# Activation sums and split widths in the second MLP product of a talking-heads kernel

## Chip, cores and metric

One core of a Trainium2 chip runs the whole program. The metric is the device time of one execution in microseconds, the median of the timed runs.

## What is computed

Four batches (b) of attention with 12 heads, 448 positions and head width 64, whose scores and weights are mixed over the heads, are followed by a leaky MLP on the 1792 rows:

```python
scores = einsum('bhij,hg->bgij', q @ k.T / 8, w_pre)
attn = exp(scores - max); attn = attn / (sum(attn) + 1e-9)
x = einsum('bhij,hg->bgij', attn, w_post) @ v        # rows b*S, columns 768
h = x @ w_in                                         # 768 -> 2048
out = maximum(0.01 * h, h) @ w_out                   # 2048 -> 768
```

## The kernel before

Everything is float32, transposed: features lie on the 128 partitions, the 448 positions of a batch are the columns. Attention runs first (some 460 us) and leaves x in DRAM (`x_dram`), while the MLP weights are unpacked into `w_dram`.

**The MLP works on pairs of batches** (p = 0 with batches 0 and 1, p = 1 with 2 and 3). Each product of a pair is a 2 x 2 block product done with seven sub-products in place of eight (names 1 to 7, in the order 1, 2, 6, 7, 5, 4, 3), whose operands are sums and differences of blocks. Each sub-product is made in float32 precision from rounded parts: `split` (L355) has ScalarE copy an operand into a high part (`wh`, `gh`, `xh`, ...; a CAST, L359) and VectorE subtract to get the low part (`wl`, `gl`, `xl`; L360). `three` (L413) then issues three matmuls: low weights by high data, high by low, high by high. 

**First product** (`hidden`, L446): eight steps j, each with seven sub-products of 9 matmuls. Weights of a step (`wi`, L382) are combined and split in parts a, s, b, d, c (`prep_wi`, L388): `wa` for sub-products 1 and 2, `wb` for 6 and 7, `wc` for 5 and 3, `wd` for 4. `keep` (L439) applies the leaky activation on ScalarE and leaves four blocks of activations g per step, in tiles of 448 columns. In pair 0, `combine_wo` (L480) has GpSimd form the four sums of the second product's weights from a load `so` and store them to `s_dram`.

**Second product** (`project`, L534): 56 steps n (seven sub-products by eight j), 9 matmuls each (three output blocks c, three matmuls). `load_wo` (L495) loads 128 x 384 weights; `prep_out` (L507) splits them and the activations of step n + 2, and has GpSimd form the five sums of activations that the later sub-products use, one block of 448 columns at a time (L517 to L526, 40 in a pair). Three buffers hold the split activations `gs`, three the split weights. In pair 0 the x blocks of pair 1 are loaded, summed and split on VectorE between the steps (`load_x` L346, `prep_x` L363, called from step 4 on).

**What sets the order.** Matmuls stay in program order (`mm`, L159); everything else is ordered by the scheduler's estimate when the program is built, and each engine then works its own list in that order. All DMAs named here are issued by SP, also in order: an issue that waits holds up those behind it. Pools opened by `open_work` (L335) take the memory of those it closes, so their first writes wait for the last readers there.

## Time and profile before

| what | us |
|---|---|
| three timed runs | 937.64, 938.81, 945.68 (median 938.81) |
| profiled execution | 934.08 |
| its span, first to last instruction | 932.4 |

The profile is that of one execution; its stages are read by the time at which they begin and end on TensorE. PE is TensorE's matmuls, PEld its weight loads, DVE VectorE, ACT ScalarE, POOL GpSimd, SPq the queue of SP.

### The profile page before, as it was taken

Reading aid. Unit: us, or ns where it says so; the run is one execution under the profiler, and the core shown is the slowest. Engines: PE = TensorE matmul, PEld = TensorE weight load, DVE = VectorE, ACT = ScalarE, POOL = GpSimd, SP = SyncE. Lnnn points to the kernel's source line nnn. Section 1 sums busy time; section 2 is a strip of 40 time slices with the busy share of each in tenths; the row PEclk is TensorE's granted clock in tenths of the full one; section 3 lists DMA queues with packets and bytes.
Section 4 is the critical chain, followed back from the end, with each engine's and each line's share of the span. In section 5 each row is a group of like instructions: output and inputs, shape, how many; then the busy total and the mean of one; then the engine's idle time right before and its main releaser. Section 6 shows DMA issues by size and latency. Waiting matters only on the chain.

```text
span 932.4 us, 18211 instructions
## 1 busy us (share of the span) xinstructions
PE 867.1 (93%) x6712; PEld 674.9 (72%) x6712; DVE 687.0 (74%) x1234; ACT 516.4 (55%) x1167; POOL 305.4 (33%) x278
## 2 busy tenths in 40 slices
PE   7999999999999999997798999778999999977998
PEld 3557757666666666665787899556889999965997
DVE  4688878787787878888857665998685655498665
ACT  3576666656666766664434554535655545442654
POOL 2133432333332333334644431782000110198000
PEclk8999999999999999999789999999999999999999
DMA  7878778877698786866555523334451122223343
GB/s 186 232 240 264 218 222 247 277 223 235 214 280 247 232 239 212 262 200 195 184 180 202 170 68 112 106 98 124 134 169 54 53 68 68 60 74 101 106 138 118
DMA packets 111081, 158.75 MB, mean 170 GB/s; under 512 B 37180, under 2 KB 95632, under 8 KB 110992
## 3 DMA queue, kind: packets, MB, share of 16 engines
q1 hardware_dynamic: 109660, 156.04, 54.7%
q10 hardware_dynamic: 1236, 1.53, 0.5%
q8 instruction: 53, 0.87, 0.4%
q14 instruction: 36, 0.29, 0.1%
q0 software_dynamic: 96, 0.01, 0.0%
HBM read 88.09 MB, written 29.88 MB: 127 GB/s over the span
## 4 chain that ended last, share of the span: by engine, by line
PE 63%; DVE 14%; DMA 10%; ACT 5%; issue 5%; POOL 3%; SPq 1%; DVEq 0%; ACTq 0%; POOLq 0%
PE pso L160 26%; PE psa L160 10%; PE pss L160 8%; PE psh L160 7%; PE psx L160 6%; PE psm L160 5%; DVE gl L360 3%; DVE wl L360 3%; DMA craw<-in_w_moe 2%; ACT et L246 2%; DMA so<-w_dram 2%; DMA xr<-x_dram 1%; DVE xl L360 1%; DMA w_dram<-w 1%; DMA wi<-w_dram 1%
## 5 line engine op out<-in xcount | busy, mean ns | idle before, releaser
L160 PEld LDWEIGHTS psa<-kp,et 128*128 128x128 f32 (+1 forms) x1840 | 158.3, 172 | 77.2 <-ACT st L212 28.2
L160 PE MATMUL psa<-kp,et 128*128 128x120 f32 (+1 forms) x1840 | 178.7, 261 | 8.9 <-DVE at L290 3.9
L119 POOL TENSOR_TENSOR w<-w,exp 128x384 f32<-128x384 f32 x64 | 66.0, 1032 | 266.3 <-issue 93.9
L160 PE MATMUL pso<-gl,wh 128*128 128x448 f32 x336 | 127.9, 381 | 18.6 <-DVE gl L360 18.6
L246 ACT ACTIVATE et<-psm,stat 128x448 f32<-128x448 f32 x184 | 115.8, 634 | 49.8 <-DVE stat L245 49.3
L160 PE MATMUL pso<-gh,wl 128*128 128x448 f32 x336 | 125.2, 373 | 10.1 <-ACT xh L359 4.4
L160 PE MATMUL pso<-gh,wh 128*128 128x448 f32 x336 | 124.1, 369 | 0.0
L245 DVE TENSOR_REDUCE stat<-psm 128x1 f32<-128x448 f32 x184 | 105.7, 616 | 17.0 <-PE psm L160 16.7
L360 DVE TENSOR_TENSOR wl<-wo,wh 128x384 fp32r<-128x384 f32 x112 | 86.0, 773 | 41.9 <-ACT wh L359 41.8
L160 PE MATMUL pss<-kt,qt 64*64 64x448 f32 (+2 forms) x768 | 109.7, 567 | 5.7 <-ACT st L212 3.9
L359 ACT CAST wh<-wo 128x384 fp32r<-128x384 f32 x112 | 57.2, 513 | 102.9 <-PE pso L160 77.2
L160 PE MATMUL psm<-r,kpre 64*64 64x448 f32 (+1 forms) x736 | 100.6, 552 | 4.6 <-DMA r<-st 4.6
L212 ACT ACTIVATE st<-pss 120x448 f32<-120x448 f32 (+1 forms) x141 | 71.8, 545 | 50.5 <-PE pss L160 49.2
L160 PEld LDWEIGHTS pso<-gl,wh 128*128 128x128 f32 x336 | 63.9, 190 | 34.6 <-DVE gl L360 29.6
L290 DVE COPY at<-psa 128x480 f32<-128x480 f32 (+1 forms) x112 | 70.3, 632 | 19.8 <-PE psa L160 19.5
L160 PEld LDWEIGHTS pso<-gh,wl 128*128 128x128 f32 x336 | 64.0, 190 | 19.6 <-ACT gh L359 5.9
L360 DVE TENSOR_TENSOR gl<-g,gh 128x448 fp32r<-128x448 f32 x96 | 78.1, 815 | 0.0
L160 PE MATMUL psx<-at,vt 128*64 128x120 f32 (+1 forms) x1152 | 66.7, 266 | 5.5 <-ACT st L212 3.1
L160 PEld LDWEIGHTS pso<-gh,wh 128*128 128x128 f32 x336 | 64.0, 191 | 4.8
L160 PEld LDWEIGHTS psm<-r,kpre 64*64 64x64 f32 (+1 forms) x736 | 33.6, 136 | 44.5 <-issue 38.6
L120 POOL TENSOR_TENSOR w<-w,top 128x384 f32<-128x384 f32 x64 | 64.0, 1000 | 5.0
L160 PEld LDWEIGHTS psx<-at,vt 128*64 128x64 f32 x1152 | 58.0, 139 | 6.9 <-ACT st L212 3.8
(129 smaller groups left out, 1586.3 us busy)
## 6 DMA issues: line engine op xcount, KB each, us to landing
r<-st SPq DMA_DIRECT2D x182, 210.0 KB
craw<-in_w_moe SPq DMA_DIRECT2D x64, 384.0 KB
w_dram<-w SPq DMA_DIRECT2D x64, 192.0 KB
wi<-w_dram SPq DMA_DIRECT2D x32, 384.0 KB
wo<-s_dram SPq DMA_DIRECT2D x64, 192.0 KB
wo<-w_dram SPq DMA_DIRECT2D x48, 192.0 KB
so<-w_dram SPq DMA_DIRECT2D x16, 384.0 KB
s_dram<-sw SPq DMA_DIRECT2D x8, 768.0 KB
```

Source lines behind the costliest of these rows:

```text
L119: pin(nc.gpsimd.tensor_mul(w, w, self.exp.bitcast(F32)))
L120: pin(nc.gpsimd.tensor_add(w, w, self.top.bitcast(F32)))
L160: pin(nc.tensor.matmul(*args, **kw))
L212: nc.scalar.activation(to, ps[:m, :S], AF.Copy, scale=scale)
L245: nc.vector.tensor_reduce(st[:, 0, g:g + 1], ps[:, :S], axis=AX.X, op=ALU.max, negate=True)
L246: nc.scalar.activation(e, ps[:, :S], AF.Exp, bias=st[:, 0, g:g + 1], accum_out=st[:, 1, g:g + 1])
L290: copy(at[:, :, QUAD * sg[0]:QUAD * sg[0] + w], ps[:, :nh * w].rearrange("p (h w) -> p h w", h=nh))
L359: hold(nc.scalar.copy(hi, raw))
L360: hold(nc.vector.tensor_sub(lo, raw, hi.bitcast(F32)))
```

## The change

- The activations of two steps j lie in one tile of 2 x 448 columns (`keep`), and a step of the second product takes two j: 28 steps of 18 matmuls, with splits of 768 and 896 columns, two weight loads a step and two buffers each for `wr`, `w` and `gs` (one step ahead).
- The sums of activations are made by VectorE in 896 columns: one of the four in the first product (after sub-product 3 of every odd j), three behind the splits of sub-products 1, 2 and 6. GpSimd has none.
- In the first product of pair 0 (after j = 1, 3, 5) the x blocks of pair 1 are loaded, summed on VectorE (`combine_x`) and stored to `xq_dram`; in the second product `load_part` and `prep_part` load and split one of 21 blocks per step, three ahead.
- In the first product `wb` is split for sub-products 6, 7 and 5 at once (1152 columns), 4 and 3 have pools of their own (`w4`, `w3`) on the right side, where `gs` lies later.
- At the end of pair 0's second product parts b, d and c of the first weights follow; part a and s are placed at steps 16 and 20. `c` tiles have four buffers and not five.

```diff
         name, raw = ((1, x[0][0]), (2, x[1][0]), (5, t), (7, x[0][1]), (6, t), (3, x[1][1]), (4, x[1][0]))[k]
         x_t[name, c] = split(pl["xs"][X_PARTS * c + k >= XS], "x", raw, hold)
 
+    X_NAMES = (1, 2, 5, 7, 6, 3, 4)
+
+    def combine_x(c):
+        x = [[xr_t[1, c, h, e] for e in range(2)] for h in range(2)]
+        t = pl["xr"].tile([P, S], F32, tag="xr", name="xt")
+        sub = nc.vector.tensor_sub
+        sub(t, x[0][1], x[0][0])
+        nc.sync.dma_start(xq_dram[c][:, 0], t)
+        sub(x[0][1], x[1][1], x[0][1])
+        nc.sync.dma_start(xq_dram[c][:, 1], x[0][1])
+        sub(x[1][1], x[1][1], t)
+        nc.sync.dma_start(xq_dram[c][:, 2], x[1][1])
+        sub(x[1][0], x[1][0], x[1][1])
+        nc.sync.dma_start(xq_dram[c][:, 3], x[1][0])
+
+    def load_part(c, k):
+        if c >= HC:
+            return
+        name = X_NAMES[k]
+        t = xr_t[1, c, k] = pl["xr"].tile([P, S], F32, tag="xr", name="xr")
+        if name < 4:
+            src = x_dram[2 + (name == 3)][:, c + HC * (name > 1)]
+        else:
+            src = xq_dram[c][:, (5, 7, 6, 4).index(name)]
+        nc.sync.dma_start(t, src)
+
+    def prep_part(c, k):
+        x_t[X_NAMES[k], c] = split(pl["xs"][X_PARTS * c + k >= XS], "x", xr_t.pop((1, c, k)))
+
     def load_wi(j):
         t = pl["wi"].tile([P, 2, 2, HALF_IN], F32, tag="r", name="wi")
         for m in range(2):
...
             hold(nc.vector.tensor_sub(s[:, 0], s[:, 2], w[:, 0, 0]))
         if part == "b":
-            two = split(pl["wb"], "wb", wi_t["s"][:, :2], hold)
-            s_t2[6], s_t2[7] = (two, 0), (two, 1)
+            two = split(pl["wb"], "wb", wi_t["s"][:, :3], hold)
+            s_t2[6], s_t2[7], s_t2[5] = (two, 0), (two, 1), (two, 2)
         if part == "d":
             s = wi_t["s"]
             hold(nc.vector.tensor_sub(s[:, 3], w[:, 0, 1], s[:, 0]))
-            s_t2[4] = split(pl["wd"], "wd", w[:, 1, 1:], hold), 0
+            s_t2[4] = split(pl["w4"], "wd", w[:, 1, 1:], hold), 0
         if part == "c":
-            two = split(pl["wc"], "wc", wi_t["s"][:, 2:], hold)
-            s_t2[5], s_t2[3] = (two, 0), (two, 1)
+            s_t2[3] = split(pl["w3"], "wc", wi_t["s"][:, 3:], hold), 0
 
     def three(ps, w, x, first, last):
 
...
         return pl[pool].tile([P, 512], F32, tag=tag, name="psh" if pool == "ps_h" else "pso")
 
     def keep(j, m, e, h):
-        g = g_t[j, m, e] = pl["g"].tile([P, S], F32, tag=f"g{m}{e}", name=f"g{m}{e}", bufs=NJF)
-        nc.scalar.activation(g, h, AF.Prelu, alpha=0.01)
+        if j % 2 == 0:
+            g_t[j // 2, m, e] = pl["g"].tile([P, 2, S], F32, tag=f"g{m}{e}", name=f"g{m}{e}", bufs=NJF // 2)
+        nc.scalar.activation(g_t[j // 2, m, e][:, j % 2], h, AF.Prelu, alpha=0.01)
 
     NJF = NF // 2
...
         if k == 3:
             product(3, hid[1], False)
             keep(j, 0, 1, hid[1][:, :S])
+            if j % 2:
+                g = g_t[j // 2, 0, 1]
+                nc.vector.tensor_sub(g, g_t[j // 2, 1, 1], g)
...
 
     ORDER = (1, 2, 6, 7, 5, 4, 3)
-    STEPS = len(ORDER) * NJF
+    NG = NJF // 2
+    STEPS = len(ORDER) * NG
 
     def load_wo(n):
         if n >= STEPS:
             return
-        k, j = ORDER[n // NJF], n % NJF
-        t = wo_t[n] = pl["wr"].tile([P, HALF_IN], F32, tag="r", name="wo")
-        if k in (1, 2, 4):
-            src = w_dram[2 * j + (k != 1)][:, DM + HALF_IN * (k == 4):][:, :HALF_IN]
-        else:
-            at = (5, 7, 6, 3).index(k)
-            src = s_dram[j][:, HALF_IN * at:HALF_IN * (at + 1)]
-        nc.sync.dma_start(t, src)
+        k, i = ORDER[n // NG], n % NG
+        t = wo_t[n] = pl["wr"].tile([P, 2, HALF_IN], F32, tag="r", name="wo")
+        for u in range(2):
+            j = 2 * i + u
+            if k in (1, 2, 4):
+                src = w_dram[2 * j + (k != 1)][:, DM + HALF_IN * (k == 4):][:, :HALF_IN]
+            else:
+                at = (5, 7, 6, 3).index(k)
+                src = s_dram[j][:, HALF_IN * at:HALF_IN * (at + 1)]
+            nc.sync.dma_start(t[:, u], src)
 
     def prep_out(n):
         if n >= STEPS:
             return
-        k, j = ORDER[n // NJF], n % NJF
-        wq_t[n] = split(pl["w0" if n % 3 == 0 else "w1"], "w", wo_t.pop(n))
-        g = {(m, e): g_t[j, m, e] for m in range(2) for e in range(2)}
-        t = g[{1: (0, 0), 2: (1, 0), 7: (0, 1), 5: (0, 0), 4: (1, 0), 3: (1, 1)}.get(k, (0, 0))]
-        sub = nc.gpsimd.tensor_sub
+        k, i = ORDER[n // NG], n % NG
+        wq_t[n] = split(pl["w"], "w", wo_t.pop(n))
+        b11, b12, b21, b22 = (g_t[i, m, e] for m in range(2) for e in range(2))
+        gs_t[n] = split(pl["gs"], "g", {1: b11, 2: b21, 6: b11, 7: b12, 5: b11, 4: b21, 3: b22}[k])
+        if k == 1:
+            nc.vector.tensor_add(b11, b12, b11)
+        if k == 2:
+            nc.vector.tensor_sub(b21, b21, b11)
         if k == 6:
-            t = pl["t"].tile([P, S], F32, tag="t", name="gt")
-            sub(t, g[1, 1], g[0, 0])
-        gs_t[n] = split(pl["gs"], "g", t)
-        if k == 1:
-            sub(g[0, 0], g[0, 1], g[0, 0])
-        if k == 2:
-            sub(g[0, 1], g[1, 1], g[0, 1])
-        if k == 7:
-            sub(g[1, 0], g[1, 0], g[1, 1])
-        if k == 5:
...
     def project(p, n):
-        k, j = ORDER[n // NJF], n % NJF
+        k, i = ORDER[n // NG], n % NG
         own = 2 if k in (2, 7, 4) else 1
         fresh = k in (1, 2, 7)
         w, g = wq_t.pop(n), gs_t.pop(n)
-        for c in range(HC):
-            if fresh and j == 0:
+        for u, c in ((u, c) for u in range(2) for c in range(HC)):
+            first, last = fresh and i == u == 0, i == NG - 1 and u == 1
+            if first:
                 o_b[own, c] = bank("ps_o", f"b{own}")
             ps = o_b[own, c]
-            three(ps[:, :S], [t[:, c * P:(c + 1) * P] for t in w], g, fresh and j == 0, j == NJF - 1)
-            if j < NJF - 1:
+            three(ps[:, :S], [t[:, u, c * P:(c + 1) * P] for t in w], [t[:, u] for t in g], first, last)
...
                     load_wi((j + 2) % NJF)
-        open_work(
-            gs=("left", 3), w0=("left", 1), wr=("right", 3), w1=("right", 2), t=("right", 2),
-        )
-        for n in range(3):
-            load_wo(n)
-        for n in range(2):
-            prep_out(n)
+            if not p and j % 2 and j < 2 * HC:
+                load_x(1, j // 2)
+                combine_x(j // 2)
+        open_work(wr=("left", 2), w=("left", 2), gs=("right", 2))
+        load_wo(0)
+        load_wo(1)
+        prep_out(0)
+        again = p + 1 < B // 2
+        if again:
+            for k in range(3):
+                load_part(0, k)
         for n in range(STEPS):
-            load_wo(n + 3)
-            prep_out(n + 2)
+            load_wo(n + 2)
+            prep_out(n + 1)
             project(p, n)
-            if p + 1 == B // 2:
-                continue
-            c, at = divmod(n - 4, 16)
-            if 0 <= c < HC and at == 0:
-                load_x(p + 1, c)
-            if 0 <= c < HC and at > 1 and at % 2 == 0:
-                prep_x(p + 1, c, at // 2 - 1)
-            if n == 30:
+            if again and n < X_PARTS * HC:
+                load_part(*divmod(n + 3, X_PARTS))
+                prep_part(*divmod(n, X_PARTS))
+            if again and n == 16:
                 prep_wi(0, "a")
-            if n == 36:
+            if again and n == 20:
                 prep_wi(0, "s")
-            if n == 42:
-                prep_wi(0, "d")
-        if p + 1 < B // 2:
-            open_work(wb=("right", 1), wc=("right", 1))
+        if again:
+            open_work(wb=("right", 1), w4=("right", 1), w3=("right", 1))
             prep_wi(0, "b")
+            prep_wi(0, "d")
             prep_wi(0, "c")
             load_wi(1)
```

Three places in the order. First, VectorE at the seam from the first to the second product of pair 0 before: `wdl` is the last weight work of the first product, `wl` and `gl` are the splits of the second product, `g_6281` is a block of activations (those of its first three steps have been split earlier in the list).

```order
L433 TENSOR_TENSOR c<-cp,psh 128x448
L360 TENSOR_TENSOR wl<-wo,wh 128x384
L433 TENSOR_TENSOR c<-cu,pso 128x448
L360 TENSOR_TENSOR wdl<-wi,wdh 128x384
L360 TENSOR_TENSOR wl<-wo,wh 128x384 x3
L360 TENSOR_TENSOR gl<-g_6281,gh 128x448
L360 TENSOR_TENSOR wl<-wo,wh 128x384
L360 TENSOR_TENSOR gl<-g_6400,gh 128x448
L360 TENSOR_TENSOR wl<-wo,wh 128x384
L360 TENSOR_TENSOR gl<-g_6519,gh 128x448
```

The same seam after: L509 is the sum in the first product of the last two j, `gl` of `g_5927` is that of step 0, `xl` are x blocks of pair 1, L551 the sums behind sub-product 1's splits.

```order
L509 TENSOR_TENSOR g_6769<-g_6732,g_6769 128x896
L361 TENSOR_TENSOR gl<-g_5927,gh 128x896
L361 TENSOR_TENSOR gl<-g_6179,gh 128x896
L361 TENSOR_TENSOR xl<-xr,xh 128x448
L551 TENSOR_TENSOR g_5927<-g_6013,g_5927 128x896
L361 TENSOR_TENSOR xl<-xr,xh 128x448 x2
L551 TENSOR_TENSOR g_6179<-g_6265,g_6179 128x896
L361 TENSOR_TENSOR xl<-xr,xh 128x448 x5
L361 TENSOR_TENSOR wl<-wo,wh 128x768
L361 TENSOR_TENSOR gl<-g_6431,gh 128x896
L361 TENSOR_TENSOR xl<-xr,xh 128x448 x2
L551 TENSOR_TENSOR g_6431<-g_6517,g_6431 128x896
```

The first splits of activations of the second product have moved behind the sum of the last activations, and eight `xl` and two sums stand between those of step 1 and those of step 2.

Second, VectorE in sub-products 1 and 2 of pair 1 before:

```order
L360 TENSOR_TENSOR wl<-wo,wh 128x384
L360 TENSOR_TENSOR gl<-g_8643,gh 128x448
L360 TENSOR_TENSOR wl<-wo,wh 128x384
L360 TENSOR_TENSOR gl<-g_8753,gh 128x448
L360 TENSOR_TENSOR wl<-wo,wh 128x384
L360 TENSOR_TENSOR gl<-g_8863,gh 128x448
L360 TENSOR_TENSOR wl<-wo,wh 128x384
L360 TENSOR_TENSOR gl<-g_8970,gh 128x448
```

and after, where L551 and L553 are sums:

```order
L361 TENSOR_TENSOR wl<-wo,wh 128x768
L361 TENSOR_TENSOR gl<-g_8390,gh 128x896
L551 TENSOR_TENSOR g_8390<-g_8467,g_8390 128x896
L361 TENSOR_TENSOR wl<-wo,wh 128x768
L361 TENSOR_TENSOR gl<-g_8607,gh 128x896
L551 TENSOR_TENSOR g_8607<-g_8684,g_8607 128x896
L361 TENSOR_TENSOR wl<-wo,wh 128x768
L361 TENSOR_TENSOR gl<-g_8009,gh 128x896
L553 TENSOR_TENSOR g_8009<-g_8009,g_7956 128x896
```

Each step has one `wl`, one `gl` and one sum of twice the width; of GpSimd's list, which had 80 sums of activations in these stages, none is left.

Third, SP in the first product of pair 0 before: `so` are loads for GpSimd's sums of weights, `s_dram` their stores, `wi` the loads of the first product's weights.

```order
L490 DMA s_dram_78<-sw 128x1536
L483 DMA so<-w_dram_66 128x768
L483 DMA so<-w_dram_67 128x768
L490 DMA s_dram_79<-sw 128x1536
L385 DMA wi<-w_dram_64 128x768
L385 DMA wi<-w_dram_65 128x768
L483 DMA so<-w_dram_68 128x768
L483 DMA so<-w_dram_69 128x768
```

and after, where `xr` are loads of x for `combine_x` and `xq_dram` its stores:

```order
L415 DMA wi<-w_dram_66 128x768
L415 DMA wi<-w_dram_67 128x768
L352 DMA xr<-x_dram_89 128x448 x2
L352 DMA xr<-x_dram_90 128x448 x2
L523 DMA s_dram_78<-sw 128x1536
L516 DMA so<-w_dram_66 128x768
L516 DMA so<-w_dram_67 128x768
L390 DMA xq_dram_84<-xt 128x448
L392 DMA xq_dram_84<-xr 128x448
L394 DMA xq_dram_84<-xr 128x448
L396 DMA xq_dram_84<-xr 128x448
L415 DMA wi<-w_dram_68 128x768
L415 DMA wi<-w_dram_69 128x768
```

Four loads of x and four stores of its sums now stand among them, and the `wi` loads of the fifth step behind the four stores.

## Rows read from the trace of the kernel before

**Rows 1.** Busy time by stage, after start:length PE, PEld, DVE, ACT, POOL, clock, DMA.

```profile
467.00:578.20 111.20, 104.67 (x498) 94.99 (x498) 66.45 (x92) 51.69 (x89) 38.12 (x30) 0.97 0.42 141
578.20:707.80 129.60, 111.56 (x505) 94.00 (x504) 108.02 (x151) 67.86 (x140) 48.07 (x34) 0.99 0.41 124
707.80:810.20 102.40, 102.40 (x506) 94.57 (x504) 55.77 (x87) 53.43 (x90) 8.72 (x6) 1.00 0.20 61
810.20:928.40 118.20, 107.54 (x505) 94.65 (x503) 88.67 (x118) 57.76 (x119) 47.53 (x34) 0.99 0.35 105
```

**Rows 2.** Waits of the second product of pair 1: total us, times, longest.

```profile
PEld pso L160 <- DVE gl L360: 14.1, 13, 1.8
```

**Rows 3.** Groups of VectorE, 862 to 907 us (GpSimd at rest).

```profile
L360 DVE TENSOR_TENSOR wl<-wo,wh 128x384 fp32r<-128x384 f32 x24 | 14.0, 585 | 15.1 <-ACT wh L359 15.1
L360 DVE TENSOR_TENSOR gl<-g,gh 128x448 fp32r<-128x448 f32 x22 | 13.6, 618 | 0.0
```

**Rows 4.** Groups of VectorE, 812 to 857 us (GpSimd forms its sums).

```profile
L360 DVE TENSOR_TENSOR wl<-wo,wh 128x384 fp32r<-128x384 f32 x20 | 22.9, 1162 | 3.0 <-ACT wh L359 3.0
L360 DVE TENSOR_TENSOR gl<-g,gh 128x448 fp32r<-128x448 f32 x13 | 19.4, 1494 | 0.0
```

**Rows 5.** Busy time of these two stretches.

```profile
812.00:857.00 45.00, 34.97 (x155) 27.91 (x154) 44.19 (x39) 18.50 (x38) 40.81 (x29) 1.00 0.32 94
862.00:907.00 45.00, 45.00 (x223) 41.64 (x222) 28.89 (x52) 26.86 (x56) 2.26 (x2) 1.00 0.41 122
```

**Rows 6.** Order of time, wide splits in the first product of pair 0.

```profile
566.04 0.82 ACT L359 CAST wch<-ws 128x768 fp32r<-128x768 f32 x1
...
566.89 0.96 DVE L360 TENSOR_TENSOR wcl<-ws,wch 128x768 fp32r<-128x768 f32 x1 [1.97 <-ACT wch L359]
```

**Rows 7.** Order of time, the split of one step in pair 1.

```profile
888.27 0.37 PE L160 MATMUL pso<-gh,wl 128*128 128x448 f32 x1
...
888.47 0.51 ACT L359 CAST wh<-wo 128x384 fp32r<-128x384 f32 x1 [0.84 <-PE pso L160]
...
889.02 0.56 DVE L360 TENSOR_TENSOR wl<-wo,wh 128x384 fp32r<-128x384 f32 x1 [0.72 <-ACT wh L359]
...
889.49 0.62 DVE L360 TENSOR_TENSOR gl<-g,gh 128x448 fp32r<-128x448 f32 x1
```

**Rows 8.** Order of time, the seam from first to second product, pair 1.

```profile
810.20 0.37 PE L160 MATMUL pso<-gh,wl 128*128 128x448 f32 x1
...
810.40 0.55 ACT L441 ACTIVATE g<-psh 128x448 f32<-128x448 f32 x1 [0.59 <-PE psh L160]
```

**Rows 9.** Order of time on TensorE, second product of pair 0.

```profile
596.05 0.66 PE L160 MATMUL pso<-gh,wl 128*128 128x448 f32 x1 [3.64 <-ACT xh L359]
```

**Rows 10.** Busy time of the 4 us after that idle.

```profile
596.00:600.00 4.00, 3.95 (x11) 3.43 (x12) 4.00 (x6) 2.19 (x6) 2.46 (x2) 0.57 0.31 82
```

**Rows 11.** Chain of waits: start, us, what (two stretches of it).

```profile
449.46 7.01 DMA so<-w_dram
...
484.59 4.82 DMA wi<-w_dram
...
631.76 2.93 DMA xr<-x_dram
...
813.47 2.35 DMA wo<-w_dram
```

**Rows 12.** Order of time on TensorE, first product of pair 0.

```profile
497.92 0.47 PE L160 MATMUL pso<-xh,wcl 128*128 128x448 f32 x1 [2.70 <-DVE c L433]
```

**Rows 13.** Order of time on SP's queue, start of the first product.

```profile
438.94 0.86 SPq L483 DMA_DIRECT2D so<-w_dram  x2
...
468.84 0.52 SPq L318 DMA_DIRECT2D x_dram<-xo  x1
...
474.02 1.33 SPq L483 DMA_DIRECT2D so<-w_dram  x2
...
516.89 1.34 SPq L483 DMA_DIRECT2D so<-w_dram  x2
```

More of the change, by code (lines that the diff above doesn't have):

```diff
@@ L80 @@
     s_dram = [dram.tile([P, 2 * DM], F32, name=f"s_dram{j}") for j in range(NF // 2)]
+    xq_dram = [dram.tile([P, 4, S], F32, name=f"xq_dram{c}") for c in range(HC)]
     x_dram = [dram.tile([P, NC, S], F32, name=f"x_dram{b}") for b in range(B)]
@@ L431, in sum_of @@
     def sum_of(t, ps):
-        c = pl["g"].tile([P, S], F32, tag="c", name="c", bufs=5)
+        c = pl["g"].tile([P, S], F32, tag="c", name="c", bufs=4)
         nc.vector.tensor_add(c, t, ps[:, :S])
@@ L509, in prep_out @@
             return
-        k, j = ORDER[n // NJF], n % NJF
-        wq_t[n] = split(pl["w0" if n % 3 == 0 else "w1"], "w", wo_t.pop(n))
-        g = {(m, e): g_t[j, m, e] for m in range(2) for e in range(2)}
-        t = g[{1: (0, 0), 2: (1, 0), 7: (0, 1), 5: (0, 0), 4: (1, 0), 3: (1, 1)}.get(k, (0, 0))]
-        sub = nc.gpsimd.tensor_sub
-        if k == 6:
-            t = pl["t"].tile([P, S], F32, tag="t", name="gt")
-            sub(t, g[1, 1], g[0, 0])
-        gs_t[n] = split(pl["gs"], "g", t)
-        if k == 1:
-            sub(g[0, 0], g[0, 1], g[0, 0])
-        if k == 2:
-            sub(g[0, 1], g[1, 1], g[0, 1])
-        if k == 7:
-            sub(g[1, 0], g[1, 0], g[1, 1])
-        if k == 5:
-            nc.gpsimd.tensor_add(g[1, 0], g[1, 0], g[0, 0])
+        k, i = ORDER[n // NG], n % NG
[6 more added lines that the diff above has]
+            nc.vector.tensor_sub(b21, b21, b11)
+        if k == 6:
+            nc.vector.tensor_sub(b11, b22, b11)
     o_b, o_s = {}, {}
@@ L538, in project @@
         w, g = wq_t.pop(n), gs_t.pop(n)
-        for c in range(HC):
-            if fresh and j == 0:
+        for u, c in ((u, c) for u in range(2) for c in range(HC)):
+            first, last = fresh and i == u == 0, i == NG - 1 and u == 1
+            if first:
                 o_b[own, c] = bank("ps_o", f"b{own}")
             ps = o_b[own, c]
-            three(ps[:, :S], [t[:, c * P:(c + 1) * P] for t in w], g, fresh and j == 0, j == NJF - 1)
-            if j < NJF - 1:
+            three(ps[:, :S], [t[:, u, c * P:(c + 1) * P] for t in w], [t[:, u] for t in g], first, last)
+            if not last:
                 continue
@@ L556, in project @@
             if k == 3:
-                t = pl["g"].tile([P, S], F32, tag="c", name="c", bufs=5)
+                t = pl["g"].tile([P, S], F32, tag="c", name="c", bufs=4)
                 (nc.scalar.copy, nc.vector.tensor_copy)[c % 2](t, ps[:, :S])
@@ L699 @@
     pool = pools(mlp, "left")
-    pl.update(wd=pool("wd", 1), g=pool("g", 1), ps_o=pool("ps_o", HC, space=PSUM))
-    pool = pools(work[0], "left")
-    pl.update(so=pool("so", 1))
+    pl.update(g=pool("g", 1), ps_o=pool("ps_o", HC, space=PSUM))
+    pl.update(so=pools(work[0], "left")("so", 1))
     prep_wi(0, "d")
@@ L728 @@
                     load_wi((j + 2) % NJF)
[L729 to L735 removed]
+            if not p and j % 2 and j < 2 * HC:
[9 more added lines that the diff above has]
+                load_part(0, k)
         for n in range(STEPS):
[L737 to L738 removed]
+            load_wo(n + 2)
+            prep_out(n + 1)
             project(p, n)
[L740 to L747 removed]
+            if again and n < X_PARTS * HC:
+                load_part(*divmod(n + 3, X_PARTS))
+                prep_part(*divmod(n, X_PARTS))
+            if again and n == 16:
                 prep_wi(0, "a")
[L749 removed]
+            if again and n == 20:
                 prep_wi(0, "s")
[L751 to L754 removed]
+        if again:
+            open_work(wb=("right", 1), w4=("right", 1), w3=("right", 1))
             prep_wi(0, "b")
+            prep_wi(0, "d")
             prep_wi(0, "c")
```

1 line of the change is left out of this document (removed).

## Prediction

> **What bounds the kernel now.** I read the busy time by stage first, then what TensorE's weight loads wait for, then the groups of VectorE where GpSimd works and where it rests, and last the order of time at the seams. TensorE has work in nearly every stretch, so a gain can only come out of those in which it idles, and the stages show where these are [rows 1]. The two second products and the first product of pair 1 each have 504 matmuls (8 x 7 x 9 or 56 x 9). The undisturbed one takes 102.4 us, 0.203 us a matmul, or 3.66 us for 18. The second products take 129.6 and 118.2 us: 27.2 and 15.8 us lost. The first product of pair 0 takes 111.2 us from its second sub-product on; 495 matmuls at that pace are 100.6, so 10.6 us are lost.
>
> In the second product of pair 1 the weight loads wait for `gl`, VectorE's half of the split activations [rows 2]. The reader is to see why: while GpSimd rests, `wl` takes 585 ns and `gl` 618 [rows 3]; while GpSimd forms its sums the same instructions take 1162 and 1494 [rows 4]. In 45 us TensorE gets 155 matmuls done beside GpSimd's sums and 223 without, with VectorE busy 44.2 and 28.9 us [rows 5]. One `wl` and one `gl` cost 2.66 us there, and nine matmuls want them every 1.83 us.
>
> **The change part by part.** *Sums on VectorE.* The 80 sums of 448 columns on GpSimd (40 a pair) go; 32 of 896 columns on VectorE come (16 a pair, four of these in the first product). No row has this width. 768 columns take 0.96 us [rows 6], two of 448 take 1.24; between them I take 1.08, because 0.618 at 448 and 0.96 at 768 lie on a line that gives it, and it lies nearest to the row at 768. GpSimd then rests in both second products, so I use the undisturbed durations there.
>
> *Splits twice as wide.* A step is now 18 matmuls and has one buffer ahead. The step pattern of before [rows 7]: `wh` starts 0.20 us after the first matmul of the following step, and `gl` ends 1.64 us after that. Wide: 0.20 + `wh` 0.82 + 0.04 + `wl` 0.96 (the rows of 768 columns [rows 6]) + `gl` 1.08 = 3.10 us. It is wanted by the second matmul of the next step, at 3.66 + 0.20 = 3.86. With every wide instruction at twice the narrow one: 0.20 + 1.02 + 0.04 + 1.12 + 1.24 = 3.62, still in time; so the narrower look-ahead costs 0. A sum behind `gl` brings VectorE to 3.12 of 3.66 us a step. That cover is 0.5 us.
>
> *The seam from first to second product.* This is the new wait. `gs` now lies where the weights of the first product lay, and `gl` of step 0 stands behind the sum of the last activation (first order below). That sum waits for the activation of the last product, which starts 0.20 us after the first matmul of the second product [rows 8] and takes 0.55. Then: 0.75 + 0.04 + sum 1.0 (start to start) + `gl` 1.08 = 2.87, at TensorE 2.95, wanted at 0.20: 2.75 us, against none in [rows 8], where `gl` was made earlier. Queued behind on VectorE is the `gl` of step 1, which 3.66 us of matmuls cover. In pair 1 nothing more is late (`gl` of step 2 ends near 9.3, wanted at 10.3).
>
> In pair 0 the eight `xl` and two sums that stand between `gl` of step 1 and `wl` of step 2 count too: `gl` 1.0, eight `xl` 8 x 0.53, two sums 2.0, `wl` 0.87 (start to start), `gl` 1.08, from the start of step 0's `gl` at 1.79 on, whose own 1.0 comes first: 11.98 against 10.2 wanted, 1.8 us. Steps 2 and 3, with three `xl` and a sum between: 0.8 more. So pair 0 pays 2.75 + 1.8 + 0.8 = 5.4.
>
> After an idle of 3.64 us [rows 9] the granted clock was 0.57 in the next 4 us, its lower level for most of them, and 11 matmuls began there [rows 10], where the undisturbed pace gives 19.7: 1.7 us. The idles at the seams are shorter; the bounds are 0 and 1.7 for each. I add 1.5 us for pair 0's two long ones and 0.8 for pair 1's, about half.
>
> *x sums through DRAM.* 12 loads, 12 sums of 448 columns and 12 stores go into the first product of pair 0 (VectorE is busy 66.5 of 111.2 us there [rows 1], and the 12 x 0.62 + 4 x 1.08 = 11.8 us fit in); 21 loads replace 12 in the second product. Such a load took 2.93 us from issue to use [rows 11]; with five buffers that is one per 0.8 us (2.93 + 0.5 + 0.6 over five) against the 0.72 us that VectorE takes in the block above: up to 1 us, 0 taken. On SP the four stores of a combination wait for VectorE and stand ahead of the next weight loads (third order below).
>
> *Weights 5 beside 6 and 7; 3 and 4 alone.* Same columns, other grouping. At the end of pair 0 the wide `wb` has 3.66 us of products 1 and 2 as its cover: 0.20 + copy 0.55 + `wh` 1.15 + `wl` 1.35 (1152 columns, by the same lines) = 3.25. Without cover it costs up to 0.8; I take 0.
>
> *The start of pair 0's first product.* Two effects of opposite sign. SP now issues `wi` of the second step and the last stores of x before the first `so`; the stall of 2.70 us [rows 12] came from VectorE's weight work, which waited for a `wi` load queued behind a store of GpSimd's sums. And GpSimd's combinations leave the end of attention. But their first `so` now stands behind the last store of x, at 468.84 and not at 438.94, and they set the pace of the later `wi` loads: seven periods of 10.7 us (four from 474.02 to 516.89 [rows 13]) put the `wi` of the last step at 469 + 75 + 1 + 4.8 (a `wi` [rows 11]) = 550. It is wanted some 20 us before the first product's end at 578, near 558. Bounds: -7 (both stalls and the half clock of the start gone) to +10 (rival 2). I take -2, nearest to the row of the stall.
>
> At this place the Trainium skill speaks against the change: *SBUF — State Buffer*, section "Who interferes with whom", says that a VectorE instruction with two SBUF inputs and a GpSimd instruction that reads SBUF exclude each other for their whole length, and that the one issued first wins. The trace agrees as far as 1494 against 618 ns goes. By that rule a 1.08 or 1.35 us VectorE instruction also holds up GpSimd's combinations longer than 0.6 us ones did; no run here shows that yet. That would give rival 2's time.
>
> **The sum**, against the profiled execution (934.08 us, its span 932.4): pair 0's second product 102.4 + 5.4 + 1.5 = 109.3, -20.3; pair 1's 102.4 + 2.75 + 0.8 = 106.0, -12.2; start of the first product -2. Together -34.5: 899.6. The median of the runs shown is 938.81, 4.7 us above the profiled one; from there I get **904 us**. With 896 columns at 0.96 or 1.24 us, six such instructions in series at the seams move it by -1 to +1.5; with the clock's bounds 901 to 908; with -7 for the start 897.
>
> **The rivals.**
> 1. *VectorE becomes the bound of the first twelve steps of each second product* (those with sums). For: 3.12 of 3.66 us are taken before any hand-over between engines. Against: even doubled narrow durations give 3.6. Price: half a microsecond for 24 steps, 12 us: 916.
> 2. *The first product of pair 0 is held by GpSimd's chain.* Each of the four instructions of a combination waits for half of a wide VectorE instruction more, 4 x 0.54: period 12.9 instead of 10.7, so the last `wi` comes at 469 + 90 + 6 = 565, some 8 us after 558, and two more for the first `wo` behind it; the -2 turns into +10: 916. For: VectorE gets 11.8 us more to do just there, and SP's stores wait for it. Against: most of the time VectorE idles there.
> 3. *The slower side: the weight loads of the second product.* Two buffers, so the load for step n+2 starts when `wl` of step n ends, and two steps cannot take less than landing + 0.82 + 0.04 + 0.96 us. A `wo` took 2.35 us [rows 11]: 2.1 us a step, hidden under 3.66. It decides from a landing of 5.5 us. A pair of loads of twice that size took 7.01 beside other transfers [rows 11]; then a step is 4.42 us, 0.76 x 56 = 43 us more: 947. For: now two loads a step, and 21 loads of x among them. Against: the pair is half as large as that of 7.01, and pair 1 has no x.
> 4. *The change doesn't free VectorE* (its long times have another cause than GpSimd): the second products stay as they are, 937. Against: [rows 3] beside [rows 4].
>
> **Chances.** Forecast 0.68, its own range 897 to 911; rival 1 0.08; rival 2 0.17; rival 3 0.04; rival 4 0.03. Range 895 to 919: it holds the forecast and most of rivals 1 and 2. A measurement of this kernel tells about 1% from no change: faster is below 929.4 (forecast, rivals 1 and 2: 0.93), within 1% are rival 4 and the half of rival 3 that falls short of 948.2 (0.05), slower by more than that is its other half (0.02).
>
> **What would show it.** Right: `gl` of 896 columns near 1.08 us with GpSimd at 0 in both second products; these at 109 and 106 us; a TensorE idle of about 2.7 us at each seam, released by `gl`, and in pair 0 a second one of about 2 us some 10 us later. Wrong: idles of TensorE in every step (rival 1 if released by `gl` with VectorE full, rival 3 if `wh` waits for `wo`), or a first product of pair 0 above 112 us with ScalarE or VectorE waiting for `wi` (rival 2).

## The result, and the profile after

The changed kernel takes 904.8 us (median of 4 runs, 902.03 to 908.85) beside 940.75 for the kernel before on the same chip: ratio 0.9617, 95% interval 0.9557 to 0.9676, faster by 3.8%. The prediction was 904 us. Medians are over all timed runs of a kernel; the ratios leave out the few runs that took over 1.5% longer than the fastest of the same kernel. The profiled execution took 905.31 us (span 903.6) and is 28.8 us shorter than that of before; by stages of TensorE:

| stage | before | predicted | after | after, a second execution |
|---|---|---|---|---|
| first product, pair 0 | 111.2 | 2 less | 109.7 | 110.3 |
| second product, pair 0 | 129.6 | 109.3 | 109.9 | 109.7 |
| first product, pair 1 | 102.4 | 102.4 | 105.5 | 103.6 |
| second product, pair 1 | 118.2 | 106.0 | 106.7 | 107.1 |

The same columns as [rows 1] (the clock is the share of its full clock that TensorE was granted), a stage now reaching from the end of the last matmul before it to the end of its own last:

```profile
467.89:577.60 109.71, 103.29 (x497) 92.55 (x496) 73.45 (x107) 53.61 (x92) 39.29 (x32) 1.00 0.75 254
577.60:687.52 109.92, 105.80 (x505) 96.94 (x505) 79.67 (x92) 58.32 (x81) 0.00 (x0) 0.97 0.43 136
687.52:792.99 105.47, 104.53 (x505) 94.27 (x503) 58.09 (x89) 52.83 (x89) 0.00 (x0) 1.00 0.20 67
792.99:899.68 106.69, 104.39 (x505) 95.78 (x504) 71.91 (x77) 50.92 (x65) 0.00 (x0) 0.98 0.34 109
```

GpSimd, the fifth busy time, is at 0 from 577.6 on. VectorE's durations are those that the prediction took (0.96 us for `wl`, 1.08 for `gl`); its groups in the second product of pair 1, with busy us and ns of one behind the bar:

```profile
L361 DVE TENSOR_TENSOR gl<-g,gh 128x896 fp32r<-128x896 f32 x28 | 30.3, 1084 | 0.0
L361 DVE TENSOR_TENSOR wl<-wo,wh 128x768 fp32r<-128x768 f32 x26 | 24.9, 958 | 29.8 <-ACT wh L360 29.5
```

What is left in the second products is at the seams, the borders from the first product to the second. Pair 1, in order of time (answers to [rows 8]): TensorE's last matmul of the first product begins at 792.79, and then

```profile
793.19 0.54 ACT L471 ACTIVATE g<-psh 128x448 f32<-128x448 f32 x1 [0.62 <-PE psh L161]
...
793.77 1.09 DVE L509 TENSOR_TENSOR g<-g,g 128x896 f32<-128x896 f32 x1 [1.81 <-ACT g L471]
794.78 2.09 DVE L361 TENSOR_TENSOR gl<-g,gh 128x896 fp32r<-128x896 f32 x2
...
794.61 0.47 PE L161 MATMUL pso<-gh,wl 128*128 128x448 f32 x1 [1.46 <-ACT gh L360]
795.92 0.47 PE L161 MATMUL pso<-gl,wh 128*128 128x448 f32 x1 [0.84 <-DVE gl L361]
```

This is the predicted chain: activation 0.20 us after the end of the first product (792.99), sum 0.78, `gl` 1.79, TensorE 2.93 (2.95 in the prediction). A matmul lasts 0.36 us but the next begins after 0.20; counted from beginning to beginning, the two idles together are 2.73 us. In pair 0 they are 4.5, because ScalarE first waits 2.17 us for an x load and has further x splits in front of the last activations:

```profile
576.71 0.57 ACT L360 CAST xh<-xr 128x448 fp32r<-128x448 f32 x1 [2.17 <-DMA xr<-xq_dram]
...
579.52 0.53 ACT L471 ACTIVATE g<-psh 128x448 f32<-128x448 f32 x1
```

```profile
580.98 0.44 PE L161 MATMUL pso<-gh,wl 128*128 128x448 f32 x1 [3.22 <-ACT gh L360]
582.33 0.74 PE L161 MATMUL pso<-gl,wh 128*128 128x448 f32 x1 [0.91 <-DVE gl L361]
```

Behind both seams the granted clock was at its lower level (answers to [rows 10]):

```profile
583.00:588.00 5.00, 5.00 (x15) 4.45 (x14) 5.00 (x9) 1.88 (x5) 0.00 (x0) 0.50 0.47 141
796.50:800.00 3.50, 3.50 (x11) 3.09 (x10) 2.37 (x3) 0.00 (x0) 0.00 (x0) 0.51 0.00 0
```

In the first product of pair 0 the stall of [rows 12] is gone, and another of 2.22 us has come 34 us later. SP, ScalarE and TensorE there:

```profile
511.72 1.36 SPq L516 DMA_DIRECT2D so<-w_dram  x2
...
523.10 0.32 SPq L523 DMA_DIRECT2D s_dram<-sw  x1
523.52 1.32 SPq L516 DMA_DIRECT2D so<-w_dram  x2
524.95 0.42 SPq L415 DMA_DIRECT2D wi<-w_dram  x1
...
530.37 0.83 ACT L360 CAST wah<-wi 128x768 fp32r<-128x768 f32 x1 [4.05 <-DMA wi<-w_dram]
...
531.69 0.47 PE L161 MATMUL pso<-xh,wdl 128*128 128x448 f32 x1 [2.22 <-ACT cp L457]
```

SP issues nothing for 10 us, since the store of GpSimd's sums waits for GpSimd; the `wi` load stands behind it, and ScalarE waits 4.05 us for that load with the copy that TensorE needs queued behind. These are the periods of GpSimd's chain [rows 13], 9.7 to 12.2 us before and now 10.0 to 11.8.

### The profile page after: what moved, and what is told of

Its sections match the earlier page's. It is cut to its first block, busy times and chain, and to the rows that moved or that the text cites. A ratio compares the mean times of both kernels' runs of the same rounds, so it can differ in the third digit from the quotient of the medians.

```text
span 903.6 us, 17823 instructions
## 1 busy us (share of the span) xinstructions
PE 857.5 (95%) x6712; PEld 674.6 (75%) x6712; DVE 648.0 (72%) x1154; ACT 501.2 (55%) x1055; POOL 192.4 (21%) x198
## 4 chain that ended last, share of the span: by engine, by line
PE 62%; DMA 12%; DVE 7%; ACT 5%; POOL 3%; issue 2%; SPq 1%; ACTq 0%; DVEq 0%; POOLq 0%
PE pso L161 30%; PE psa L161 10%; PE psx L161 7%; PE pss L161 7%; PE psm L161 5%; PE psh L161 4%; DMA craw<-in_w_moe 3%; DMA wi<-w_dram 3%; DMA so<-w_dram 3%; ACT et L247 2%; DMA w_dram<-w 2%; DVE xl L361 1%; POOL sw L519 1%; POOL sw L522 1%; DVE stat L246 1%
## 5 line engine op out<-in xcount | busy, mean ns | idle before, releaser
L161 PE MATMUL pso<-gl,wh 128*128 128x448 f32 x336 | 125.1, 372 | 1.7 <-DVE gl L361 1.7
L360 ACT CAST wh<-wo 128x768 fp32r<-128x768 f32 x56 | 46.7, 837 | 89.6 <-PE pso L161 84.6
L361 DVE TENSOR_TENSOR wl<-wo,wh 128x768 fp32r<-128x768 f32 x56 | 53.5, 958 | 56.6 <-ACT wh L360 54.7
L103 ACT ACTIVATE z<-craw 128x384 f32<-128x384 f32 x64 | 35.8, 560 | 51.9 <-DMA craw<-in_w_moe 45.6
```

Of the source, the lines that this page charges most:

```text
L103: pin(nc.scalar.activation(self.z, self.high.bitcast(F32), AF.Copy, scale=2.0**-112))
L161: pin(nc.tensor.matmul(*args, **kw))
L360: hold(nc.scalar.copy(hi, raw))
L361: hold(nc.vector.tensor_sub(lo, raw, hi.bitcast(F32)))
```

## The experiments

Attention is the same in all these kernels, but its end (the start of pair 0's regular matmuls) lay anywhere between 462 and 472 us in the profiled executions. How much of the scatter of one kernel's total this is was not shown, since only the changed kernel was profiled twice (467.9 and 467.2 us). So effects of a few us are read from stages, whose lengths are TensorE's, end to end, and from the time between that start and the end of the span: 465.3 us before, 435.7 and 434.7 in the two executions of the changed kernel, and 445.8, 443.4, 427.7, 438.8, 431.5, 434.6, 422.7 and 422.4 in experiments 1 to 8, 419.4 in the tenth. Each ratio is to the kernel before on the same chip, which took 940.4 to 941.0 us everywhere.

**1. The sums back on GpSimd.**

```diff
-            nc.vector.tensor_add(b11, b12, b11)
+            nc.gpsimd.tensor_add(b11, b12, b11)
...
-            nc.vector.tensor_sub(b21, b21, b11)
+            nc.gpsimd.tensor_sub(b21, b21, b11)
...
-            nc.vector.tensor_sub(b11, b22, b11)
+            nc.gpsimd.tensor_sub(b11, b22, b11)
```

> The changed kernel with the three sums of activations of the second product (12 of 896 columns a pair) back on GpSimd; widths, steps and everything else as changed. Theory (contention: VectorE's splits and GpSimd's sums draw each other out): in the twelve steps with sums gl of 896 columns takes 1.8 to 3.0 us and not 1.08, wl 1.3 to 2.0 and not 0.96, TensorE waits for gl in these steps, and the time is 915 to 935 us beside about 905 of the changed kernel. Rival (fewer and wider steps brought the gain, whoever forms the sums): VectorE's durations or TensorE's idle hardly change and the time is within 3 us of 905.

918.4 us, ratio to before 0.9777 (0.9723 to 0.983): second products of 118.0 us (pair 0) and 109.0 (pair 1), against 109.9 and 106.7. In pair 1, VectorE and then GpSimd:

```profile
830.57 1.08 DVE L361 TENSOR_TENSOR gl<-g,gh 128x896 fp32r<-128x896 f32 x1
832.23 2.51 DVE L361 TENSOR_TENSOR wl<-wo,wh 128x768 fp32r<-128x768 f32 x1 [0.57 <-ACT wh L360]
```

```profile
831.80 2.13 POOL L553 TENSOR_TENSOR g<-g,g 128x896 f32<-128x896 f32 x1 [1.96 <-DVE gl L361]
```

The sum takes 2.13 us and `wl`, begun during it, ends 0.8 us after it: 2.51 where 0.96 is its own. In such steps `gl` is not drawn out, as it was expected to be, because the sum waits for it. The step lasts 4.09 us against 3.66. In pair 0 six `xl` beside two of the sums take 7.12 us from 584.76 on (in the changed kernel five took 2.86), ScalarE then waits 3.69 and 2.00 us for x loads, and TensorE has its longest idle of the stage:

```profile
598.21 0.71 PE L161 MATMUL pso<-gh,wl 128*128 128x448 f32 x1 [5.39 <-DVE wl L361]
```

The sums on GpSimd cost 13.6 us by the medians and 10.4 by these two stages; but the kernel keeps 22 of the 36 us gained although GpSimd still forms three sums in four.

**2. The kernel before with its narrow sums on VectorE.**

```diff
-        sub = nc.gpsimd.tensor_sub
+        sub = nc.vector.tensor_sub
...
-            nc.gpsimd.tensor_add(g[1, 0], g[1, 0], g[0, 0])
+            nc.vector.tensor_add(g[1, 0], g[1, 0], g[0, 0])
```

> The kernel before with its 80 sums of 448 columns on VectorE and not on GpSimd; steps of 9 matmuls, widths and x as before. Theory (GpSimd's rest is the gain, the width brings little): gl 0.62 and wl 0.59 us throughout, VectorE 1.55 us (start to start) of the 1.83 of a step, second product of pair 1 at 102.5 to 105 us (before 118.2), of pair 0 at 104 to 112 (before 129.6), the time 903 to 912 us. Rival (the width is needed because three narrow instructions and their hand-overs fill a step of 1.83 us): second product of pair 1 at 108 us or more, of pair 0 at 118 or more, the time 917 us or more.

918.7 us, ratio 0.9763 (0.9715 to 0.9811): 116.3 us in pair 0, 108.5 in pair 1. The durations were as the theory has them (`gl` 619 ns), but the time and pair 1's stage were the rival's; pair 0's stage lies between the two. In pair 1 VectorE does 30 of the 40 sums between 800 and 836 us, beside 20 `wl`, almost without a gap, and TensorE waits for it in the third step of sub-product 6:

```profile
833.22 0.47 PE L160 MATMUL pso<-gh,wl 128*128 128x448 f32 x1 [0.31 <-ACT gh L359]
835.16 0.74 PE L160 MATMUL pso<-gl,wh 128*128 128x448 f32 x1 [1.48 <-DVE gl L360]
```

About half of the 6.2 us that this stage takes over TensorE's pace are such idles; behind them the granted clock was 0.76 (833 to 840 us).

**3. The seam: two pools for the split activations**, so that step 0's lie where only earlier sub-products' weights were.

```diff
-        gs_t[n] = split(pl["gs"], "g", {1: b11, 2: b21, 6: b11, 7: b12, 5: b11, 4: b21, 3: b22}[k])
+        gs_t[n] = split(pl["gsb" if n % 2 else "gsa"], "g", {1: b11, 2: b21, 6: b11, 7: b12, 5: b11, 4: b21, 3: b22}[k])
...
-        open_work(wr=("left", 2), w=("left", 2), gs=("right", 2))
+        open_work(wr=("left", 2), w=("left", 2), gsa=("right", 1), gsb=("right", 1))
```

> The changed kernel with the two buffers of split activations as two pools of one buffer each, so that gh and gl of step 0 lie where only weights of earlier sub-products were and are made before the last activation; the sum of the last activations then comes behind gl of step 0. Theory (the seam's idle is the wait of gl of step 0 for the memory and the sum, and the low clock behind it comes from that idle): no TensorE idle over 0.5 us at the seam of pair 1 and no stretch at the lower clock behind it, 4.4 us gained there (2.7 of idle, 1.7 of clock); at pair 0's seam 4 to 7 us gained; the time 893 to 898 us beside 905. Rival (the wait only moves to gl of step 1 or to the x splits on ScalarE): the time 902 to 906.

899.5 us, ratio 0.9565 (0.9514 to 0.9615), between the two expectations. Pair 1's stage is TensorE's own pace, with no idle and full clock:

```profile
793.05:895.35 102.30, 102.30 (x505) 94.39 (x503) 70.21 (x76) 50.07 (x64) 0.00 (x0) 1.00 0.35 113
```

So the seam cost 4.4 us there, as expected. In pair 0 only 2.1 us were gained (107.8) and not 4 to 7: the seam's idle is 0, and VectorE is now late behind it, for `gl` of step 1, which the prediction had covered by matmuls, and in step 3, where it had step 2. The longer seam had covered both (TensorE):

```profile
587.03 0.48 PE L161 MATMUL pso<-gl,wh 128*128 128x448 f32 x1 [1.28 <-DVE gl L361]
595.61 0.44 PE L161 MATMUL pso<-gh,wl 128*128 128x448 f32 x1 [1.21 <-DVE wl L361]
596.52 0.47 PE L161 MATMUL pso<-gl,wh 128*128 128x448 f32 x1 [0.47 <-DVE gl L361]
```

**4. No x through DRAM** (the four loads of a `c`, sums and splits in the second product, as before).

```diff
-            if not p and j % 2 and j < 2 * HC:
-                load_x(1, j // 2)
-                combine_x(j // 2)
...
-                load_part(*divmod(n + 3, X_PARTS))
-                prep_part(*divmod(n, X_PARTS))
+                c, at = divmod(n - 2, 8)
+                if at == 0:
+                    load_x(p + 1, c)
+                else:
+                    prep_x(p + 1, c, at - 1)
```

> The changed kernel without x through DRAM: nothing of pair 1's x in the first product; in the second product of pair 0 four loads of a c at once, its sums and splits on VectorE one part a step (from step 2 on, 8 steps a c), as the kernel before does. Theory (the x loads, sums and stores of the first product hold up SP's weight loads, and the x splits ahead of the last activations lengthen pair 0's seam): the stalls of TensorE between 529 and 546 us, 5 us together, shrink to under 2, pair 0's seam costs as much as pair 1's (4.4 us and not 7.4), the time 896 to 900 us beside 905. Rival (x through DRAM pays, since its sums and its wait for loads would stall the second product as the 3.64 us idle of before): new idles of 2 us or more in the second product of pair 0, the time 905 to 910.

911.6 us, ratio 0.9699 (0.965 to 0.9747), above both expectations. Half of the theory held: pair 0's seam has the 2.7 us of pair 1. But new idles released by `gl` and `wl`, of 0.4 to 1 us, come behind it (113.3 us in all), and the first product's stall got longer. SP, ScalarE and TensorE there:

```profile
513.58 0.32 SPq L523 DMA_DIRECT2D s_dram<-sw  x1
514.00 1.33 SPq L516 DMA_DIRECT2D so<-w_dram  x2
515.44 0.98 SPq L415 DMA_DIRECT2D wi<-w_dram  x2
...
522.21 0.83 ACT L360 CAST wah<-wi 128x768 fp32r<-128x768 f32 x1 [6.17 <-DMA wi<-w_dram]
...
523.53 0.74 PE L161 MATMUL pso<-xh,wdl 128*128 128x448 f32 x1 [4.40 <-ACT cp L457]
```

Without any transfer of pair 1's x `wi` is just as late behind GpSimd's store: x's traffic is not the cause. So x through DRAM pays: the kernel without it takes 6.8 us more by the medians and 3.1 more from the start of pair 0.

**5. The x splits held, one a step,** behind `gh` and `gl` of the following step (`of_g` holds these two instructions).

```diff
+                with tc.issue_after(of_g[0].ins), tc.issue_after(of_g[1].ins):
-                prep_part(*divmod(n, X_PARTS))
+                    prep_part(*divmod(n, X_PARTS))
```

> The changed kernel with each of the 21 x splits of pair 0's second product held in the order behind gh and gl of the following step, one a step, so that none stands ahead of the last activations or between the first splits. Theory (the x splits ahead of ScalarE's last activations, waiting for their loads, made pair 0's seam longer than pair 1's): the idle at that seam falls from 4.5 us (3.4 and 1.15) to the 2.7 of pair 1, the second product of pair 0 from 109.9 to 106 to 107.5 us, the time 901 to 903 beside 905. Rival (the twelve steps with sums then hold wl, gl, an x split and a sum, 3.4 us start to start of 3.66, and VectorE becomes their bound): idles of TensorE released by gl in most of these steps, the second product of pair 0 at 110 to 114 us, the time 905 to 909.

899.3 us, ratio 0.9565 (0.9493 to 0.9637). Second product of pair 0 at 107.0 us, its seam now that of pair 1 (a second idle of 0.82 us, released by `gl`, follows at 576.24):

```profile
574.98 0.44 PE L161 MATMUL pso<-gh,wl 128*128 128x448 f32 x1 [1.51 <-ACT gh L360]
```

One idle of 0.41 us is left in the twelve steps, so VectorE does not become their bound.

**6. GpSimd issues its own loads and stores.**

```diff
-            nc.sync.dma_start(raw[:, m].rearrange("p k n -> p (k n)"), w_dram[2 * j + m][:, DM:])
+            nc.gpsimd.dma_start(raw[:, m].rearrange("p k n -> p (k n)"), w_dram[2 * j + m][:, DM:])
...
-        nc.sync.dma_start(s_dram[j], s.rearrange("p k n -> p (k n)"))
+        nc.gpsimd.dma_start(s_dram[j], s.rearrange("p k n -> p (k n)"))
```

> The changed kernel with the loads and stores of GpSimd's weight sums (so, s_dram) issued by GpSimd itself and not by SP, so that no wi load stands behind a store that waits for GpSimd. Theory (the stalls of TensorE in the first product of pair 0 between 529 and 546 us, 5 us together, are SP waiting for GpSimd's chain): they shrink to under 1.5 us, that stage from 109.7 to 104 to 106.5 us, the time 899 to 902 beside 905. Rival (the wi loads wait for their one buffer or for x's stores, not for GpSimd): the stalls stay and the time is 904 to 907.

903.7 us, ratio 0.961 (0.9544 to 0.9676): no change in total (and 434.6 us from the start of pair 0, against 435.7 and 434.7), though the stalls between 529 and 546 us are gone (first product 107.1 us; two of 0.98 and 0.85 us at 488 and 567 are there instead). What was gained there came back at the seam, of 5.8 us now: the first `wo` load was issued only at 571.12, and `wl` of step 0 came late.

**7. Edits 3 and 5 together.**

> The changed kernel with both the two pools for the split activations (gl of step 0 made before the last activation) and the x splits held behind gl of the following step, one a step. Theory (all that is lost in the second products is the seam and the x splits that stand between the first splits): both second products at TensorE's pace, 102.3 us in pair 1 and 102.3 to 104 in pair 0, the time 892 to 896 beside 905. Rival (VectorE is full in the first twelve steps of pair 0, so the x splits cost there what they cost at the seam): second product of pair 0 at 106 us or more, the time 897 to 900.

897.9 us, ratio 0.9552 (0.9475 to 0.9629). The total is the rival's (897 to 900), the stages are the theory's: both second products run at TensorE's pace, within 0.6 us:

```profile
572.06:674.90 102.84, 102.42 (x506) 94.59 (x504) 80.20 (x97) 59.84 (x85) 0.00 (x0) 1.00 0.51 156
...
778.51:880.82 102.31, 102.31 (x505) 94.40 (x503) 70.20 (x76) 50.08 (x64) 0.00 (x0) 1.00 0.35 113
```

**8. Edits 3, 5 and 6 together.**

> The changed kernel with all three: two pools for the split activations, x splits held one a step, and GpSimd's weight sums with a queue of their own. Theory (the three losses are apart in time and add up): the first product of pair 0 at 104 to 106.5 us, both second products at 102.3 to 104, the time 886 to 891. Rival (what one gives the next takes back, as when an earlier end of the first product meets weights of the second that come later): within 2 us of the kernel with the first two alone.

897.3 us, ratio 0.9526 (0.9448 to 0.9604): within a microsecond of the seventh, the rival. The first product takes 107.6 us, pair 0's second product 104.6: its seam waits for `wl` 1.5 us.

**9. What GpSimd costs VectorE, by itself.** To the seventh kernel, in pair 1's second product, two additions a step on GpSimd whose results nothing uses.

```diff
+            if p:
+                lo = gs_t[n][1].bitcast(F32)
+                for u in range(2):
+                    t = pl["xr"].tile([P, S], F32, tag="xr", name="extra")
+                    nc.gpsimd.tensor_add(t, lo[:, 0], lo[:, 1])
```

> The kernel with two pools and held x splits, to which two additions of 448 columns on GpSimd are added in every one of the 28 steps of pair 1's second product; each reads gl of its step and its result is used by nothing. Theory (a sum on GpSimd takes its whole length out of VectorE's time and the other way round): GpSimd at rest takes 0.97 us for 384 columns start to start, so 1.13 for 448; a step then holds 0.87 + 1.0 + 1.0 + 2.26 = 5.1 us where it has a sum (12 steps) and 4.1 where not (16), against 3.66, and the second product of pair 1 goes from 102.3 us to 120 to 130. Rival (the two only slow each other somewhat, and GpSimd's 2.3 to 3 us a step fit beside VectorE's 2 to 3 in 3.66): 102.3 to 106 us.

914.9 us (one run); that stage takes 122.2 us instead of 102.3. VectorE's and GpSimd's groups from 792 to 905 us, then one step of each:

```profile
L361 DVE TENSOR_TENSOR gl<-g,gh 128x896 fp32r<-128x896 f32 x26 | 50.1, 1927 | 0.0
L361 DVE TENSOR_TENSOR wl<-wo,wh 128x768 fp32r<-128x768 f32 x26 | 42.1, 1621 | 8.3 <-ACT wh L360 8.3
...
L779 POOL TENSOR_TENSOR extra<-gl 128x448 f32<-128x448 f32 x52 | 85.3, 1660 | 30.4 <-DVE gl L361 30.4
```

```profile
815.62 1.09 DVE L556 TENSOR_TENSOR g<-g,g 128x896 f32<-128x896 f32 x1
816.63 1.91 DVE L361 TENSOR_TENSOR wl<-wo,wh 128x768 fp32r<-128x768 f32 x1
818.46 2.04 DVE L361 TENSOR_TENSOR gl<-g,gh 128x896 fp32r<-128x896 f32 x1
...
825.34 1.14 DVE L462 TENSOR_TENSOR c<-cp,pso 128x448 f32<-128x448 f32 x2
```

```profile
815.66 3.88 POOL L779 TENSOR_TENSOR extra<-gl 128x448 f32<-128x448 f32 x2 [1.03 <-DVE gl L361]
...
825.50 1.15 POOL L779 TENSOR_TENSOR extra<-gl 128x448 f32<-128x448 f32 x1 [1.03 <-DVE gl L361]
```

The step from `gl` to `gl` is 4.92 us (TensorE's waits for `gl` end at 800.89, 805.81 and so on), 4.01 in steps without a sum; expected were 5.1 and 4.1 if one engine stands while the other works. The last rows show the exception: beside VectorE's additions with one input in PSUM (`c`) an `extra` took 1.15 us, and these took no longer than elsewhere. This is what the Trainium skill says (*SBUF — State Buffer*, section "Who interferes with whom"): VectorE with two SBUF inputs and a reading GpSimd exclude each other; with at most one SBUF input, outside VectorE's two-port modes, they don't. The trace agrees to within 0.2 us a step (4.92 for 5.1, 4.01 for 4.1).

**10. Edits 3, 5 and 6, and the x loads behind `wo` on SP** (`last_wo` holds the last load of `wo`; the first three x loads are held in the same way).

```diff
+                with tc.issue_after(last_wo[0].ins):
-                load_part(*divmod(n + 3, X_PARTS))
+                    load_part(*divmod(n + 3, X_PARTS))
```

> The kernel with all three edits (two pools, held x splits, GpSimd's own queue), with the x loads of the second product also held behind the weight loads wo of their step on SP. Theory (with a queue of its own the seam of pair 0 waited for wo loads that stood behind x loads): no idle at that seam, the second product of pair 0 at 102.3 to 103 us (104.6 without the hold), the first product of pair 0 107 to 108 us from its first undisturbed product, the time 893 to 897. Rival (the wo loads are late for another reason, the memory of GpSimd's sums that they take): 104 to 106 us there and no change of the time.

892.2 us (6 runs, 884.74 to 900.19), ratio 0.9492 (0.9441 to 0.9544), the lowest median, though its interval overlaps those of the seventh and the eighth; from the start of pair 0 it is 3.0 us below the eighth. The first product took 105.1 us, better than expected: the eighth's idles of 1.37 and 1.40 us at 488 and 567 are not there, and why is not shown. Pair 0's second product took 104.1, the rival's value. GpSimd, SP and TensorE at that seam:

```profile
564.48 0.56 POOL L523 DMA_DIRECT2D s_dram<-sw  x1 [0.30 <-POOL sw L522]
...
568.48 1.75 SPq L543 DMA_DIRECT2D wo<-w_dram  x4
...
573.58 0.47 PE L161 MATMUL pso<-gh,wl 128*128 128x448 f32 x1 [0.97 <-DVE wl L361]
```

`wo` now waits for nothing on SP's queue but for the memory of GpSimd's sums, whose last store was issued 4.0 us earlier; the profile names that store as what ended SP's wait of 5.8 us. That this memory is the rest of the seam was not tried by itself.

**11. The changed kernel again, on the tenth's chip.**

> The changed kernel once more, on the same chip as the kernel with all edits and the held weight loads, so that the two can be set side by side: 901 to 908 us, with second products of 109 to 111 us (pair 0) and 106 to 107 (pair 1). If the differences between the variants were the chip's and not the kernels', it would come within 3 us of that kernel.

906.6 us, ratio 0.9629 (0.9587 to 0.9671): 14 us above the tenth, and the stages above in the table. So the difference between these two is the kernels' and not the chip's.

## Why the prediction was right, and where it was not

- *VectorE is held by GpSimd's sums.* Right, and shown by the ninth experiment. The prediction was one-sided, though: it put the whole gain down to GpSimd's rest and counted the wider steps as 0. Of the 31.2 us gained in the two second products, the first experiment, which leaves the sums on GpSimd, keeps 20.8; the second, which has narrow steps and the sums on VectorE, gains 23.0. Either part alone does most of it. The count behind it: where one excludes the other their times add up, and before, 40 sums of 1.15 us (the ninth experiment's) and 56 steps' splits of 0.47 and 0.54 (start to start) make 103 us of a stage of 102.4; TensorE had to wait. Twelve sums of 2.13 and 28 steps of 0.87 and 1.0 make 78. On VectorE the same sums make 64. Narrow steps with all sums on VectorE stay 14 us short of the changed kernel by the medians, 8.2 by the two stages. What of the first experiment's gain is width and what the smaller number of sums (24 of the old width for 40) was not separated, nor what the other handling of x does in pair 0.
- *Durations of 896 columns.* Right: 1.084 and 1.09 for the assumed 1.08 (the line that the prediction names gives 1.10), and VectorE kept up in every step behind the seams of the profiled execution (rivals 1 and 3 did not happen: `wl` waits for `wh`, and `wh` for TensorE's buffers, never for `wo`, in either second product).
- *The seam of pair 1.* Right to 0.02 us in its chain, and the third experiment shows that nothing else was lost in that stage. The clock's term was mis-sized: 0.8 us taken, some 1.7 measured, its upper bound.
- *The seam of pair 0.* The sum came out (109.9 for 109.3), the steps did not. "Up to 1 us, 0 taken" for the x loads failed: ScalarE's wait for one of them and the splits in front of the last activations lengthened the seam from 2.75 to 4.5 us, and the clock cost some 3 and not 1.5. The 2.6 us of catch-up did not show, since the longer seam at half clock gave VectorE that time; once the seam was gone, they came out as 2.1 (1.37 and 0.71 over the pace), and 1.45 more at step 1, where none was predicted. Two errors of opposite sign cancelled.
- *The start of pair 0's first product.* Its end came 0.6 us earlier, not 2: attention ended 0.8 us later (467.89 against 467.08) and the stage was 1.4 shorter. Half of rival 2's mechanism is there: the periods of GpSimd's chain hold `wi`, and the stalls between 529 and 546 us are some 5 us. But the periods did not grow to the 12.9 that it assumed (10.9 on average for 10.7), since GpSimd's sums of weights did not get slower (1.25 us on average before, 1.24 after), and the stage did not get longer. x's stores on SP, which the prediction also named, are not behind it (fourth experiment).
- *The wide `wb` at the end of pair 0.* "Without cover it costs up to 0.8; I take 0": 0.92 and 0.34 us here, and about 0.9 for the first in every kernel with the wide `wb`. The copy waits behind the splits on ScalarE; this term should have been taken. The first of them on TensorE:

```profile
692.08 0.47 PE L161 MATMUL psh<-xh,wbl 128*128 128x448 f32 x1 [0.76 <-ACT cp L457]
```

- *The sum.* 899.6 was predicted on the scale of the profiled execution, and 905.31 measured. The 5.7 between them, to rounding: 3.1 in the first product of pair 1 (1.3 `wb`, some 1.8 a slower pace of matmuls, below), 1.4 at the start, 1.3 in the second products. The medians agree to 1 us because the 4.7 us added for the median of before were not found again after. The forecast's cause is right as far as it goes and its size is right; the last 5 us of agreement are luck. Three slips in its working change nothing here: -7 for the start gives 899 and not 897, 565 is 7 us behind 558 and not 8, and eight `xl` with two sums make 0.78 us a block and not 0.72.

## What to carry to other kernels

A sum of two SBUF tiles moved from VectorE to GpSimd is not taken off VectorE while VectorE itself works on two SBUF inputs: it took 1.15 us of it here, for 448 columns, where VectorE's own took 0.54, so count both engines' times as one sum and hold it against the stage. Where tiles reuse memory at the border of two stages, look at what was there last: splitting one pool of two buffers into two pools of one let the first split go ahead and gave back the whole seam of pair 1 (4.4 us). An unheld prefetch can move ahead of work that the bound engine waits for; holding it behind that work gave 2.9 us of pair 0's second product. A queue that waits for a slow engine delays what another engine needs; here a queue of its own for GpSimd removed those stalls but, by itself, nothing of the total.
